# The w_in stage in blocks of 768 tokens instead of 576: matmuls of 384 columns, 24 units, sums of x in place, a new timetable

## The chip, the cores and the metric

The kernel runs on one core of one Trainium2 chip. The metric is the time of one execution on the device, in microseconds (us); of several runs the median counts. Engines: PE is TensorE (PEld its weight loads), DVE VectorE, ACT ScalarE, POOL GpSimd, and SP is SyncE, which in this kernel mostly issues transfers.

## The reference, cut to what matters

Three parts follow one another: linear attention, a mixture of eight experts with one expert for each token, and a dense layer pair with a silu between. The change lies in the first half of the last part.

```python
h = x @ w_in                          # x: 2304 x 512, w_in: 512 x 2048
g = h * (1.0 / (1.0 + np.exp(-h)))
return (g @ w_out).astype(np.float32)  # w_out: 2048 x 512
```

## The kernel before

**Precision.** Every product is computed from two fp32r parts, "high" and "low", of each operand: ScalarE's copy rounds to the high part, VectorE subtracts for the low part. One product of a 128 x 128 weight tile is three matmuls (`three`, L819 to L822: high x high, high x low, low x high).

**Stages.** First comes the attention, then the expert stage in slots s = 0 to 21, each of 128 tokens: `mm1` in four steps, `relu`, a turn through the identity on TensorE (`hturn`), `mm2` in four steps. For each step ScalarE and VectorE split a part of the weights. The outputs of the slots go to the scratch `yd`. Then the w_in stage, and last the w_out stage, which this text calls the drain.

**The w_in stage** multiplies by a scheme like Strassen's, with 7 products for a 2 x 2 split of blocks. The tokens come in 4 blocks k of 2 x TN = 576; the columns of w_in in NJP = 8 pairs q. A unit u = 8k + q is one pair on one block, 32 units in all. Its 7 products (`prod(u, n)`, n from 1 to 7) have six matmuls of TN = 288 columns each. Products 1, 6, 7 and 4 add up in bank puA, 5 and 3 in puC, 2 in puB. After some of the products ScalarE copies puA into an h tile (`keep`, L1121), and VectorE adds puC or puB onto an h tile (`join`, L1128); each finished h tile is stored to the scratch `hd` through SyncE's queue.

A block of x passes through these steps: `xfetch` loads tiles of 128 tokens (on SyncE for tokens in order, on GpSimd by index for the others), `xscale` multiplies by the gate, `xprep` turns a tile by four transposes into one bank and copies it to `xf`; `xsum` builds on VectorE the sums T1n, T2n, T3 and T4 that the scheme needs; `xsplit` is a high part on ScalarE (L1084) and a low part on VectorE (L1088) for each of B11, B21, B22 and T1n to T4. Weights pass through `wfetch` (load), `whigh` (L1015, 1792 elements a partition) and `wlow` (L1019).

**The conversion of w_out** runs beside it. w_out comes as 64-bit floats; `oload` loads one raw tile of 512 KB, `owork` is called four times for the steps that narrow it to 32 bits on VectorE, `okeep` and `osums` build the seven combinations that the drain needs, and `ostore` sends them through GpSimd's queue to the scratch `woscr` (L1195). Later `ofetch` (L1207) loads them from there, and `ohigh` (L1212) and `olow` split them.

**Order.** In this stage each engine works in program order. `unit(u)` issues the products 1 and 5 of u, 4 of u - 1, 6 of u, 3 of u - 1, then 2 and 7 of u. After each, it issues what the timetable `plan()` has put there: `at(u, n, f, ...)` means "after product n in unit u". So "(7,1)" below is the place after product 1 in unit 7. The list `TAIL` is the same for the last expert slot: its entries 0 to 3 are issued with the four steps of mm1 of slot 21, entries 4 to 7 with those of mm2(21). The prods (0,1), (0,5), (0,2), (1,1) and (1,5) follow, and `first_units` has the rest of units 0 and 1. A conditional block, `rest()`, for tokens that don't fit the slots, is skipped on these inputs.

Of the kernel before, what the change touches and what calls it, by code (L numbers as in the profile page):

```python
# [19 lines left out]
P = 128  # L20
# [13 lines left out]
TN = 288  # L34
# [31 lines left out]
def moe_kernel(ctx, tc, qk, v, w_phi, emb, tau, w1, w2, win, wout, out):  # L66
# [193 lines left out]
    def phase_all(ctx):  # L260
# [741 lines left out]
        BK = {}  # L1002

# [37 lines left out]
        def xprep(k, n):  # L1041
            i = tiles_of(k)[n]
            if n == 0:
                XF[k] = [sp.tile([P, 4, TN], F32, name="xf") for _ in range(2)]
# [15 lines left out]
        def xsum(k, name):  # L1060
            b11, b21, b12, b22 = parts(k)
            s = X.setdefault(("s", k), {"B11": b11, "B21": b21, "B22": b22})
            two = lambda nm: b11 if k == 0 else pools["ur"].tile([P, 2, TN], F32, tag="xf2", name="xf2", bufs=2)
            if name == "T1n":
                s[name] = b11
                nc.vector.tensor_tensor(out=b11, in0=b11, in1=b12, op=ALU.subtract)
            elif name == "T3":
                s[name] = b12
                nc.vector.tensor_tensor(out=b12, in0=b22, in1=b12, op=ALU.subtract)
            else:  # L1070
                a, b = (s["T1n"], b22) if name == "T2n" else (s["T2n"], b21)
                s[name] = two(name)
                nc.vector.scalar_tensor_tensor(out=s[name], in0=a, scalar=-1.0, in1=b, op0=ALU.mult,
                                               op1=ALU.subtract)

        def xhigh(k, name):
            if name == "B11":
                pool, tag = (pools["ur"], "xcB") if k % 2 else (sp, "xcA")
            else:
                pool, tag = sp, "xc" + name  # L1080
            s = X.setdefault(("s", k), dict(zip(("B11", "B21", None, "B22"), parts(k))))
            xc = pool.tile([P, 2, 2, TN], F32R, tag=tag, name=tag, bufs=1)
# [7 lines left out]
        def xsplit(k, name):  # L1090
# [75 lines left out]
        def wspot(dt=F32, name="ws"):  # L1166
            return pools["ul"].tile([P, 1536], dt, tag="ws", name=name, bufs=3)

        def oload(j):
            t = wspot(name="wo")  # L1170
            J[NJ + j] = [t[:, 0:1024].bitcast(I32).rearrange("p (f t) -> p f t", t=2), t[:, 1024:1536].bitcast(I32), t]
# [7 lines left out]

        def okeep(m):  # L1180
            ta, tb = J[NJ + m][2], J[NJ + NJP + m][2]
            J["o", m] = {0: ta[:, 1024:1280], 1: tb[:, 1024:1280], 6: tb[:, 1280:1536]}
            ostore(m, 0, 1, 6)

        def osums(m):
            ta, tb = J.pop(NJ + m)[2], J.pop(NJ + NJP + m)[2]
            b11, b12, b21, b22 = (t[:, 1024 + n * 256:1280 + n * 256] for t in (ta, tb) for n in range(2))
# [46 lines left out]
        def gspace0():  # L1234
            for r in range(2):
                gspace(wspot(name="g0"), (0, r))
# [36 lines left out]
        def hspace(t):  # L1273
            if t < 5:
                tags = (("ws", "xcA"), ("xf", "xf"), ("xcT1n", "xcB21"), ("xcT2n", "xcT3"), ("xcT4", "xcB22"))[t]
                two = [wspot(F32R, "hl0") if tag == "ws" else
                       sp.tile([P, 4 * TN], F32R, tag=tag, name="hlx", **({} if tag == "xf" else {"bufs": 1}))
                       for tag in tags]
                HB.append([x[:, 0:1024] for x in two])
# [72 lines left out]
        def rest():  # L1352
            t0, hs = wspot(name="fr0"), wspot(name="fr1")[:, 0:1024]
            t1 = wspot(F32R, "fr2")
            xr, rw = t0[:, 0:512], t0[:, 512:1024]
            ch_, cl_, xh_ = (t1[:, i * 512:(i + 1) * 512] for i in range(3))
            xl_ = pools["ur"].tile([P, 2, TN], F32R, tag="xf2", name="fr3", bufs=2).rearrange("p a t -> p (a t)")[:, 0:512]
            for s in range(NSF, NS):
# [39 lines left out]
                nc.scalar.dma_start(out=yd[bass.ds(r, P), :], in_=xr)  # L1398
        slots = ExitStack()
# [180 lines left out]
        late = ExitStack()  # L1580
        cload(CA)
        cload(CA + 1)
        for s in range(1, NSF + 1):
# [6 lines left out]
            if s < NSF:  # L1590
# [3 lines left out]
                for k in range(4):  # L1594
# [10 lines left out]
                    if k > 1 and 18 <= s < 21 and 2 * (s - 18) + k - 2 < 5:  # L1605
# [12 lines left out]
            if s == 17:  # L1618
# [3 lines left out]
                sp = ctx.enter_context(tc.tile_pool(name="sp", bufs=2, **T))  # L1622
                xfetch(0, 0)
                xfetch(0, 1)
            for i in range(4):
# [12 lines left out]
                if i > 1 and 18 <= s < 21:  # L1638
                    n = 2 * (s - 18) + i - 2
                    if n < 5:  # L1640
                        xprep(0, n)
                        if n < 3:
                            xfetch(0, n + 2)
                    else:
                        xsplit(0, "B11")
            if s < NSF:
                hturn(s)
            if s == NSF - 1:
                xfetch(1, 0)
                xfetch(1, 1)  # L1650
# [13 lines left out]
        pools["ul"] = ctx.enter_context(tc.tile_pool(name="ul", bufs=1, **T))  # L1664
# [11 lines left out]
        def plan():  # L1676
            for q in range(2, NJP):
                at(q - 2, 3 if q == 3 else 6, whigh, q)
                at(*((1, 2) if q == 2 else (q - 1, 5)), wlow, q)
            at(1, 4, wfetch, 6)  # L1680
            at(2, 4, wfetch, 7)
            for k in range(1, NT // (2 * TN)):
                u = NJP * (k - 1)
                for n in range(2 if u else 0):
                    at(u + 1, 1, xfetch, k, n)
                for n, (v, m) in enumerate(((2, 1), (3, 1), (3, 6), (4, 6), (5, 4))):
# [118 lines left out]
```

## Time and profile before

| | before |
|---|---|
| median of 3 runs | 887.43 us (887.1 to 887.65) |
| profiled execution, its own time | 886.14 us |
| its span | 884.4 us |
| granted TensorE clock, mean of the span | 0.998 |
| PE busy | 867.6 us (98%) |
| PEld busy | 794.0 us (90%) |
| DVE busy | 712.0 us (81%) |
| ACT busy | 609.6 us (69%) |
| POOL busy | 287.7 us (33%) |

Busy times are sums over the whole span. The profiled execution is one execution; its time is 1.7 us above its span, and it is 1.3 us under the median of the runs. In the trace the first product of the w_in stage starts at about 500 us, and the drain's first products at about 691 us.

### The profile page before, as it was taken

The page shows a single profiled execution, that of the slowest core. Times are in us where ns is not written, and L with a number is a line of the kernel's source. Part 1 is how long each engine was busy: PE and PEld are TensorE (multiplying, and loading weights), DVE is VectorE, ACT ScalarE, POOL GpSimd, SP SyncE. Part 2 cuts the span into 40 slices and gives each one's busy share as a digit, 9 for nine tenths or more (in the row PEclk, how much of TensorE's full clock was granted, in tenths as well). Part 3 has the DMA queues.
Part 4 walks back from the last instruction along what each step waited for, and adds up shares of the span by engine and source line. Part 5 has one row for each costly group of instructions (what it writes and reads, how often), then busy time and mean ns, then how long its engine had stood idle before and what let it go on. Part 6 is the DMA issues. An engine that isn't in the chain of part 4 may idle for free. (4 is left out here: it accounts for less than half of the span.)

```text
span 884.4 us, 17109 instructions
## 1 busy us (share of the span) xinstructions
PE 867.6 (98%) x6087; PEld 794.0 (90%) x6087; DVE 712.0 (81%) x1165; ACT 609.6 (69%) x999; POOL 287.7 (33%) x298
## 2 busy tenths in 40 slices
PE   8999999999999999999999999999999999999996
PEld 6999999988677778888888899999999999999996
DVE  6888888897898999999988957776765697676761
ACT  6877888746877889889888765444346676656551
POOL 6888887712401523105210021433310001011011
PEclk9999999999999999999999999999999999999999
DMA  6456363449596696877598495788869864726220
GB/s 188 129 141 188 99 186 99 130 132 368 204 238 218 219 252 203 300 247 187 157 369 316 165 304 180 247 289 274 280 211 311 278 170 125 208 76 170 74 81 37
DMA packets 138314, 178.07 MB, mean 201 GB/s; under 512 B 35720, under 2 KB 98824, under 8 KB 138224
## 3 DMA queue, kind: packets, MB, share of 16 engines
q1 hardware_dynamic: 122944, 143.01, 50.9%
q0 software_dynamic: 15200, 33.89, 13.7%
q8 instruction: 49, 0.80, 0.4%
q14 instruction: 41, 0.34, 0.1%
q10 hardware_dynamic: 80, 0.03, 0.0%
HBM read 174.01 MB, written 55.18 MB: 259 GB/s over the span
## 5 line engine op out<-in xcount | busy, mean ns | idle before, releaser
L870 DVE TENSOR_TENSOR wl<-raw,wh 128x1024 fp32r<-128x1024 f32 (+1 forms) x166 | 187.8, 1172 | 19.1 <-ACT wh L869 12.7
L869 ACT CAST wh<-raw 128x1024 fp32r<-128x1024 f32 (+1 forms) x166 | 162.4, 1026 | 20.2 <-PE ph L822 7.6
L1121 ACT COPY ht<-puA 128x288 f32<-128x288 f32 x128 | 50.6, 400 | 80.6 <-PE puA L822 68.4
L447 POOL TENSOR_TENSOR kl<-ke,kh 128x640 fp32r<-128x640 f32 (+1 forms) x52 | 76.7, 1491 | 22.8 <-ACT kh L443 21.7
L820 PE MATMUL ph<-wh,xh 128*128 128x512 f32 x166 | 67.1, 404 | 0.6 <-ACT xh L874 0.6
L822 PE MATMUL ph<-wh,xl 128*128 128x512 f32 x166 | 65.0, 392 | 0.9 <-DVE xl L877 0.9
L821 PE MATMUL ph<-wl,xh 128*128 128x512 f32 x166 | 64.8, 391 | 0.0
L498 PE MATMUL pnx<-kv,qp 128*128 128x73 f32 x512 | 62.3, 275 | 0.0
L822 PE MATMUL pdA<-wod,hlx 128*128 128x256 f32 x216 | 61.2, 283 | 0.6 <-DVE hlx L1287 0.6
L405 DVE TENSOR_REDUCE m<-pqk 128x10 f32<-128x1280 f32 (+1 forms) x32 | 43.4, 1358 | 21.5 <-PE pqk L398 21.3
L498 PEld LDWEIGHTS pnx<-kv,qp 128*128 128x128 f32 x512 | 59.9, 192 | 0.3
L431 ACT ACTIVATE ke<-d 128x640 f32<-128x640 f32 (+1 forms) x52 | 35.6, 684 | 29.9 <-POOL vl L421 15.4
L398 PE MATMUL pqk<-wbd,zh 128*128 128x256 f32 x288 | 53.8, 286 | 1.0 <-DVE d L406 0.9
L1128 DVE TENSOR_TENSOR ht<-puC,ht 128x288 f32<-128x288 f32 x64 | 29.0, 453 | 31.7 <-PE puC L822 25.4
L1195 POOL DMA_DIRECT2D woscr<-wo x56 | 30.8, 557 | 64.3 <-DVE wo L221 61.4
L855 POOL DMA_INDIRECT xg<-xd,gidx x22 | 28.2, 1283 | 68.9 <-PE pxt L890 30.0
L391 POOL TENSOR_TENSOR zl<-z,zh 128x512 fp32r<-128x512 f32 (+1 forms) x29 | 41.6, 1433 | 25.5 <-ACT zh L385 24.6
L820 PE MATMUL pdA<-wod,hlx 128*128 128x256 f32 x176 | 49.8, 283 | 0.0
L821 PE MATMUL pdA<-wod,hlx 128*128 128x256 f32 x176 | 49.8, 283 | 0.0
L1031 POOL DMA_INDIRECT yt<-yd,yidx x13 | 15.2, 1165 | 100.1 <-DMA hd<-ht 69.0
L398 PEld LDWEIGHTS pqk<-wbd,zh 128*128 128x128 f32 x288 | 44.7, 190 | 2.8 <-issue 2.2
L406 DVE TENSOR_TENSOR d<-pqk,m 128x1280 f32<-128x1280 f32 (+1 forms) x32 | 43.5, 1358 | 1.1
(467 smaller groups left out, 3013.2 us busy)
## 6 DMA issues: line engine op xcount, KB each, us to landing
raw<-w SPq DMA_DIRECT2D x44, 1536.0 KB
raw<-w SPq DMA_DIRECT2D x44, 512.0 KB
hd<-ht SPq DMA_DIRECT2D x124, 144.0 KB
wo<-wout SPq DMA_DIRECT2D x16, 512.0 KB
gb<-hd SPq DMA_DIRECT2D x16, 512.0 KB
woscr<-wo POOLq DMA_DIRECT2D x56, 128.0 KB
yd<-ys SPq DMA_DIRECT2D x23, 256.0 KB
z<-qk SPq DMA_DIRECT2D x16, 320.0 KB
```

The source lines that it names most:

```text
L391: eng.tensor_tensor(out=zl, in0=z, in1=zh.bitcast(F32), op=ALU.subtract)
L398: nc.tensor.matmul(out=pqk[:, c * 256:(c + 1) * 256], lhsT=z[:, c * P:(c + 1) * P], rhs=wbd[:, j].rearrange("p h f -> p (h f)"), start=(i ...
L405: nc.vector.tensor_reduce(out=m, in_=pv[:, 0:2 * n], axis=AX.X, op=ALU.max, apply_absolute_value=True)
L406: nc.vector.tensor_tensor(out=d.rearrange("p c s f -> p (c s) f"), in0=pv[:, 0:2 * n], in1=m.unsqueeze(2).to_broadcast([P, 2 * n, F]), op= ...
L447: nc.gpsimd.tensor_tensor(out=kl[:, :, s, :], in0=st.pop(("ke", g, s)), in1=kh[:, :, s, :].bitcast(F32), op=ALU.subtract)
L498: nc.tensor.matmul(out=pn[:, c, 0:73], lhsT=qp[:, s, c * P:(c + 1) * P], rhs=kv[:, s, g % 2, 0:73], start=(s == 0), stop=(s == 1))
L820: nc.tensor.matmul(out=o, lhsT=ah, rhs=bh, start=first, stop=False, skip_group_check=more)
L821: nc.tensor.matmul(out=o, lhsT=ah, rhs=bl, start=False, stop=False, skip_group_check=more)
L822: nc.tensor.matmul(out=o, lhsT=al, rhs=bh, start=False, stop=last, skip_group_check=more)
L869: nc.scalar.copy(out=hi[:, 0:n], in_=sl[:, 0:n])
L870: nc.vector.tensor_tensor(out=lo[:, 0:n], in0=sl[:, 0:n], in1=hi[:, 0:n].bitcast(F32), op=ALU.subtract)
L1121: nc.scalar.copy(out=htile(u, at), in_=BK[u, "A"])
```

## The change

- TN becomes 384: 3 blocks of 768 tokens, 24 units, matmuls of 384 columns. A block of x now is 6 whole tiles.
- `xsum` writes in place: T1n and T4 to one buffer (the one of the raw x tiles, YT), T3 over B12, T2n over B11. Each split part of x has one buffer. `xf` and YT get pools of their own, h tiles are 8 instead of 11.
- The list TAIL and the timetable are written anew. B11 of the first block is split in TAIL and not before; T4 and B22 are split after prods in units 0 and 1.
- The raw tiles of w_out were 3 in rotation; now there is one for each half, and the narrowed parts have three small buffers. `osums` still writes into the raw tile of the second half.
- `rest()` moves from ahead of unit 5 to ahead of unit 2. Block 1 of x was begun in the last expert slot on SyncE and GpSimd; it is now fetched whole in the stage.

```diff
-TN = 288
+TN = 384
 def xfetch(k, n):
-            yt = sp.tile([P, DM], F32, name="yt")
+            yt = YT[0][:, n % 2 * DM:(n % 2 + 1) * DM]
 def xsum(k, name):
-            two = lambda nm: b11 if k == 0 else pools["ur"].tile([P, 2, TN], F32, tag="xf2", name="xf2", bufs=2)
+            aside = YT[0][:, 0:2 * TN].rearrange("p (c t) -> p c t", c=2)
+            s[name] = {"T1n": aside, "T3": b12, "T2n": b11, "T4": aside}[name]
...
 def xhigh(k, name):
-                pool, tag = (pools["ur"], "xcB") if k % 2 else (sp, "xcA")
+            xc = xhome(name).tile([P, 2, 2, TN], F32R, tag="xc" + name, name="xc" + name, bufs=1)
...
-        TAIL = [[(whigh, 0), (xsum, 0, "T1n")], [(wlow, 0), (xsplit, 0, "T1n")], [(xsplit, 0, "B21"), (whigh, 1)],
-                [(xsum, 0, "T2n"), (wlow, 1)], [(xsplit, 0, "T2n"), (xsum, 0, "T3")], [(xsplit, 0, "T3")],
-                [(xsum, 0, "T4"), (xsplit, 0, "T4")], [(xsplit, 0, "B22")]]
+        TAIL = [[(whigh, 0), (xsplit, 0, "B11")], [(wlow, 0), (xsum, 0, "T1n")], [(xsplit, 0, "T1n")],
+                [(xsplit, 0, "B21"), (whigh, 1)], [(wlow, 1), (xsum, 0, "T2n")], [(xsplit, 0, "T2n"), (xsum, 0, "T3")],
+                [(xsplit, 0, "T3")], [(xsum, 0, "T4")]]
...
-                HT[u, at] = pools["ur"].tile([P, TN], F32, tag="h", name="ht", bufs=11)
+                HT[u, at] = pools["ur"].tile([P, TN], F32, tag="h", name="ht", bufs=8)
...
 def wspot(dt=F32, name="ws"):
-            return pools["ul"].tile([P, 1536], dt, tag="ws", name=name, bufs=3)
+            return pools["ul"].tile([P, 1024], dt, tag="ws", name=name, bufs=2)
 def oload(j):
+            if not WS:
+                WS.extend(wspot() for _ in range(2))
+                WS.extend(dspot() for _ in range(3))
+            m, second = j % NJP, j // NJP
+            t = WS[second]
...
         for u in range(2, NUNIT):
-            if u == NJP - 3:
+            if u == 2:
                 more = nc.values_load(regs[0:1, 2, NSF:NSF + 1], min_val=0, max_val=NT + P)
```

The new timetable of `plan()` (the old one stands in the function above):

```python
at(0, 6, xsplit, 0, "T4")
at(1, 6, xsplit, 0, "B22")
for q in range(2, NJP):
    at(*{2: (0, 7), 3: (1, 3)}.get(q, (q - 2, 6)), whigh, q)
    at(*((1, 7) if q == 2 else (q - 1, 5)), wlow, q)
at(1, 4, wfetch, 6)
at(2, 4, wfetch, 7)
for k in range(1, NT // (2 * TN)):
    u = NJP * (k - 1)
    at(u + 2 - k // 2, 1, xfetch, k, 0)
    at(u + 2 - k // 2, 1, xfetch, k, 1)
    for n, (v, m) in enumerate(((3, 1), (3, 6), (4, 1), (4, 6), (5, 1), (5, 6))):
        at(u + v, m, xscale, k, n)
        at(u + v, m, xprep, k, n)
        if n < 4:
            at(u + v, {1: 5, 6: 3}[m], xfetch, k, n + 2)
    for v, m, f, name in ((6, 5, xsum, "T1n"), (6, 3, xsum, "T3"), (7, 1, xsplit, "B11"), (7, 1, xsum, "T2n"),
                          (7, 5, xsplit, "T1n"), (7, 5, xsum, "T4"), (7, 6, xsplit, "T2n"),
                          (7, 2, xsplit, "B21"), (7, 7, xsplit, "T3"), (8, 4, xsplit, "T4"),
                          (8, 3, xsplit, "B22")):
        at(u + v, m, f, k, name)
tiles = [m + NJP * e for m in range(NJP) for e in range(2)]
loads = [(2, 1), (2, 4), (3, 5), (4, 7), (7, 4), (8, 4), (9, 1), (11, 1), (11, 4), (13, 1), (12, 4), (15, 1),
         (16, 6), (17, 5), (17, 6), (18, 7)]
works = [(2, 7), (3, 6), (4, 3), (5, 6), (8, 3), (9, 3), (10, 1), (11, 3), (12, 1), (13, 3), (13, 1), (16, 1),
         (17, 1), (17, 2), (18, 6), (19, 6)]
sums = {0: ((3, 2), (4, 1), (4, 5)), 1: ((5, 2), (6, 1), (6, 5)), 2: ((9, 7), (10, 6), (10, 3)),
        3: ((11, 7), (12, 6), (12, 3)), 4: ((13, 7), (14, 1), (14, 5)), 5: ((16, 4), (16, 2), (16, 7)),
        6: ((17, 7), (18, 5), (18, 4)), 7: ((19, 2), (20, 1), (20, 5))}
# oload at loads[j], four steps of owork from works[j] on, okeep, osums and ostore of the sums at sums[m]
...
for m, p in enumerate(((19, 1), (19, 4), (20, 1))):
    at(*p, ofetch, m, 0)
for m, p in enumerate(((20, 7), (21, 1), (21, 4))):
    at(*p, ofetch, m, 1)
for m in range(3):
    at(21 + m, 1, ohigh, m, 0)
    at(21 + m, 5, olow, m, 0)
    at(21 + m, 6, ohigh, m, 1)
    at(21 + m, 3, olow, m, 1)
...
```

The loads of the drain's first blocks (`gload`) move to units 20 to 22, and its buffers get a pool of their own.

## Rows read from the trace of the kernel before

**Rows 1.** Busy us (x count) by stretch; then granted clock, DMA share, GB/s.
```profile
480.00:500.00 20.00, 20.00 (x103) 16.64 (x102) 19.81 (x21) 18.59 (x25) 0.00 (x0) 1.00 0.65 234
...
560.00:580.00 20.00, 20.00 (x155) 20.00 (x155) 12.37 (x30) 7.77 (x18) 10.71 (x16) 1.00 0.93 306
```
**Rows 2.** Timeline of TensorE, w_in stage: start us, us, engine, line, operation.
```profile
645.03 0.30 PE L820 MATMUL puA<-xcB,wb 128*128 128x288 f32 x1
...
649.83 0.30 PE L820 MATMUL puA<-xcT,wb 128*128 128x288 f32 x1
```
**Rows 3.** Timeline of TensorE, mm2(20), hturn(21), mm2(21) and prod(0,5).
```profile
494.32 0.39 PE L820 MATMUL py<-wh,hh 128*128 128x512 f32 x1
...
497.27 0.39 PE L821 MATMUL py<-wl,hh 128*128 128x512 f32 x1
...
497.73 1.03 PE L922 MATMUL ht<-ident,hs 128*128 128x128 f32 x8
...
500.99 0.40 PE L820 MATMUL po<-wh,hh 128*128 128x512 f32 x1
...
501.46 0.39 PE L822 MATMUL po<-wh,hl 128*128 128x512 f32 x1
...
511.12 0.29 PE L822 MATMUL puB<-xcB,wb 128*128 128x288 f32 x1
...
511.39 0.40 PE L820 MATMUL puA<-xcT,wb 128*128 128x288 f32 x1
```
**Rows 4.** Timeline of VectorE ahead of the stage.
```profile
490.19 2.03 DVE L1019 TENSOR_TENSOR wb<-wb 128x1792 fp32r<-128x1792 f32 x1
...
492.13 0.75 DVE L1088 TENSOR_TENSOR xcT1n<-xf,xcT1n 128x576 fp32r<-128x576 f32 x1
...
496.07 4.62 DVE L870 TENSOR_TENSOR wl<-raw,wh 128x1024 fp32r<-128x1024 f32 x4
...
500.62 1.28 DVE L877 TENSOR_TENSOR hl<-ht,hh 128x512 fp32r<-128x512 f32 x2
```
**Rows 5.** Timeline of ScalarE ahead of the stage.
```profile
488.45 1.71 ACT L1015 CAST wb<-wb 128x1792 fp32r<-128x1792 f32 x1
...
490.26 0.68 ACT L1084 CAST xcT1n<-xf 128x576 fp32r<-128x576 f32 x1
...
491.42 1.69 ACT L1015 CAST wb<-wb 128x1792 fp32r<-128x1792 f32 x1
...
493.02 1.07 ACT L910 ACTIVATE hs<-ph 128x512 f32<-128x512 f32 x2
...
493.98 1.04 ACT L869 CAST wh<-raw 128x1024 fp32r<-128x1024 f32 x1
...
507.31 0.70 ACT L1121 COPY ht<-puA 128x288 f32<-128x288 f32 x2
```
**Rows 6.** Timeline of TensorE around a tile's four transposes.
```profile
562.36 0.29 PE L822 MATMUL puA<-xcB,wb 128*128 128x288 f32 x1
...
562.50 0.60 PE L1048 MATMUL pt<-ident,yt 128*128 128x128 f32 x4
...
562.85 0.38 PE L820 MATMUL puC<-xcT1n,wb 128*128 128x288 f32 x1
...
563.07 0.30 PE L821 MATMUL puC<-xcT1n,wb 128*128 128x288 f32 x1
```
**Rows 7.** Timeline of GpSimd: the stores of one m.
```profile
560.48 2.33 POOL L1195 DMA_DIRECT2D woscr<-wo  x4 [0.56 <-DVE wo L1190]
```
**Rows 8.** Timeline of SyncE: the load of the next raw tile of w_out.
```profile
567.31 0.33 SPq L169 DMA_DIRECT2D wo<-wout  x1
```
**Rows 9.** Waits of SyncE, 562 to 600 us: us in all, times, longest.
```profile
SPq L169 <- DMA woscr<-wo: 1.3, 1, 1.3
```
**Rows 10.** Timeline of SyncE: a load of w_out's combinations.
```profile
664.32 0.88 SPq L1207 DMA_DIRECT2D wob<-woscr  x2
```
**Rows 11.** Timeline of ScalarE: the cast behind that load.
```profile
669.83 1.05 ACT L1212 CAST wob<-wob 128x1024 fp32r<-128x1024 f32 x1 [0.20 <-DMA wob<-woscr]
```

More of the change, by code (lines that the diff above doesn't have):

```diff
@@ L1043, in xprep @@
             if n == 0:
-                XF[k] = [sp.tile([P, 4, TN], F32, name="xf") for _ in range(2)]
+                XF[k] = [xf_pool.tile([P, 4, TN], F32, name="xf") for _ in range(2)]
             yt = X.pop(("y", k, n))
@@ L1234, in gspace0 @@
         def gspace0():
+            ul.close()
+            xf_ctx.close()
+            dl = pools["dl"] = ctx.enter_context(tc.tile_pool(name="dl", bufs=1, **T))
             for r in range(2):
-                gspace(wspot(name="g0"), (0, r))
+                gspace(dl.tile([P, 1024], F32, name=f"g{r}"), (0, r))
+            OSB.extend(dl.tile([P, DM], F32, name=f"os{n}") for n in range(2))
         def gspace1():
@@ L1274, in hspace @@
             if t < 5:
[L1275 to L1279, printed above, removed]
+                homes = (("dl", "dl"), ("dl", "dl"), ("T1n", "B21"), ("T2n", "T3"), ("B11", "dr"))[t]
+                two = [pools[home].tile([P, 1024], F32R, name=f"hl{t}{n}") if home in pools else
+                       sp.tile([P, 4 * TN], F32R, tag="xc" + home, name="hlx", bufs=1)[:, 0:1024]
+                       for n, home in enumerate(homes)]
+                HB.append(two)
             return HB[t % 5]
@@ L1352, in rest @@
         def rest():
-            t0, hs = wspot(name="fr0"), wspot(name="fr1")[:, 0:1024]
-            t1 = wspot(F32R, "fr2")
+            t0, hs = wspot(name="fr0"), wspot(name="fr1")
             xr, rw = t0[:, 0:512], t0[:, 512:1024]
-            ch_, cl_, xh_ = (t1[:, i * 512:(i + 1) * 512] for i in range(3))
-            xl_ = pools["ur"].tile([P, 2, TN], F32R, tag="xf2", name="fr3", bufs=2).rearrange("p a t -> p (a t)")[:, 0:512]
+            ch_, cl_, xh_ = (dspot(F32R, f"fr{i}") for i in range(2, 5))
+            xl_ = xf_pool.tile([P, 2 * DM], F32R, tag="yt", name="fr5", bufs=1)[:, 0:512]
             for s in range(NSF, NS):
@@ L1639, in phase_all @@
                     n = 2 * (s - 18) + i - 2
[L1640 to L1645, printed above, removed]
+                    xprep(0, n)
+                    if n < 4:
+                        xfetch(0, n + 2)
             if s < NSF:
@@ L1691, in plan @@
-                at(u + 4, 2, xsplit, k, "B11")
-                at(u + 5, 2, xsum, k, "T1n")
-                at(u + 6, 5, xsum, k, "T2n")
-                at(u + 6, 6, xsum, k, "T3")
-                at(u + 6, 2, xsum, k, "T4")
-                for v, n, name in ((7, 5, "T1n"), (7, 6, "T2n"), (7, 2, "B21"), (7, 7, "T3"), (8, 4, "T4"), (8, 3, "B22")):
-                    at(u + v, n, xsplit, k, name)
-            units = [u for u in range(6, 25) if u not in (7, 15, 23)]
-            assert len(units) == NJ
@@ new lines, in plan @@
+            for j, ld, (u, n) in zip(tiles, loads, works):
+                at(*ld, oload, j)
+                for e, m in {3: ((0, 3), (0, 3), (0, 2), (0, 2)), 1: ((0, 1), (0, 5), (0, 4), (0, 4)),
+                             6: ((0, 6), (0, 6), (0, 3), (0, 3)), 2: ((0, 2), (0, 2), (0, 7), (0, 7)),
+                             7: ((0, 7), (0, 7), (1, 1), (1, 1))}[n]:
+                    at(u + e, m, owork, j)
+            for m, (k, a, b) in sums.items():
+                at(*k, okeep, m)
+                at(*a, osums, m)
+                at(*b, ostore, m, 2, 3, 4, 5)
@@ L1731, in phase_all @@
+            at(20, 6, gspace0)
+            at(20, 6, gload, 0, 0)
+            at(20, 3, gload, 0, 1)
+            at(20, 7, gspace1)
+            for (u, n), pr in zip(((21, 5), (21, 6), (21, 2), (22, 1)), ((1, 0), (0, 2), (0, 3), (1, 1))):
+                at(u, n, gload, *pr)
+            at(22, 1, ahead, 0)
+            at(22, 5, prepare, 0)
+            at(23, 5, prepare, 1)
+            at(23, 6, ahead, 3)
+            at(23, 2, ahead, 4)
         plan()
@@ L1737, in phase_all @@
                     rest()
+                yspace()
             unit(u, todo)
         prepare(2)
-        OSB.extend(sp.tile([P, DM], F32, tag="yt", name="os") for _ in range(2))
         dprod(0)
```

82 lines of the change are left out of this document (27 added, 55 removed).

## The prediction

> **What bounds the kernel now.** I read the busy time by stretches first, for the stretch that the change rebuilds and the one ahead of it [rows 1]. From 560 to 580 us, in the w_in stage, TensorE is busy for all 20 us, while VectorE works 12.4 us and ScalarE 7.8. From 480 to 500, where the expert stage ends and the first block of x is made ready, VectorE has 19.8 us of work and ScalarE 18.6: there all three are full at once. Then the timeline of TensorE, for the pace. Thirty-six steps of 288 columns take 649.83 - 645.03 = 4.80 us, or 0.1333 us from start to start [rows 2]; thirteen steps of 512 columns take 497.27 - 494.32 = 2.95 us, or 0.2269 [rows 3]. Outside a few gaps of some tenths the stage is this pace and nothing else. So two things decide: how the pace changes with the width, and whether ScalarE and VectorE can still keep their dates under the new order. The timelines of those two engines just before the stage [rows 4, 5] show who waits for whom there.
>
> **The matmuls.** A line through the two widths gives (0.2269 - 0.1333) / 224 = 0.000418 us per column and 0.013 us that a matmul costs whatever its width. At 384 columns that is 0.1333 + 96 x 0.000418 = 0.1734 us. Before there are 32 units of 7 products of 6 matmuls, 1344 x 0.1333 = 179.2 us; after, 24 x 42 = 1008 x 0.1734 = 174.8 us. Gain **4.4 us**. The columns in all stay the same; 336 fixed costs go. The width lies between two measured ones, so I bound the gain by 4.2 and 4.6.
>
> The Trainium skill (TensorE: Matmul & The Clock Gate, Back-to-back issue gap) gives an isolated warm matmul N/2.4 plus about 2.5 ns. By it the fixed part would be 2.5 ns, not 13, and the gain 336 x 0.0025 = 0.8 us. The rows disagree: 288 columns would start every 122.5 ns by it, and they start every 133.3.
>
> **The transposes.** A group of four that turns one tile of x starts at 562.50; the next product starts at 562.85 instead of 562.36 + 0.13, and its second matmul comes 0.22 behind the first, not 0.13 [rows 6]: 0.36 + 0.09 = 0.45 us a group. Blocks of 576 touch 5 tiles each (20 groups), blocks of 768 touch 6 (18 groups). Gain **0.9 us**. The sixth tile of the first block falls into the expert stage, so TensorE comes 0.45 later to the stage's start.
>
> **The start of the stage.** Here the new order costs. Prices first, from occupied steps: VectorE takes 1.94 us for 1792 elements (490.19 to 492.13) and 4.62 / 4 = 1.15 for 1024 [rows 4], so 0.89 for 768 and 0.50 for 384; ScalarE takes 1.60 for 1792 (491.42 to 493.02) and about 0.30 for 288 in the pair at 507.31 [rows 5], so 0.73 for 768, 0.49 for 512, 0.38 for 384.
>
> Before, the sum T1n stands in VectorE's queue ahead of the long wlow(0), so ScalarE's cast of T1n follows its whigh(0) at once, at 490.26 [rows 5]. After, the list TAIL puts the split of B11 first, then wlow(0), and T1n's sum behind it. ScalarE: whigh(0) 488.45 to 490.05, cast of B11 to 490.8. VectorE: low part of B11 to 491.75, wlow(0) to 493.7, sum T1n to 494.6. ScalarE has nothing to do from 490.8 to 494.65. Behind its T1n cast are queued the B21 cast and whigh(1) (0.73 + 0.73 + 1.60): the relu of the last slot starts at 497.7, not 493.02. Then come four casts of w2 at 0.95 (498.75 to 502.55). The first is done at 499.8; VectorE's four low parts take 4.6 more, to 504.35, and the first half of hl(21), before at 500.62 [rows 4], ends at 505.0. TensorE wants that hl in the third matmul of mm2(21), before at 501.46 [rows 3]; with 0.45 for the tile and 18 products' matmuls at 0.04 more each (0.72) it would stand there at 502.6. Loss **2.4 us**, a part of it already at the transposes of hs (497.73 before), which wait for the relu.
>
> A second wait follows on the same chain. wlow(1) and T2n's sum have moved behind hl(21). From its end (505.6): wlow(1) 1.94, sum T2n 0.89, cast 0.73, low 0.89, sum T3 0.89, cast 0.73, then in ScalarE's queue the copy of the last output (0.49) and keep(0,1) (0.38), with about 0.5 for handing over: 513.0. Only then may prod(0,6) add to its bank. TensorE is there after 22 matmuls of 0.227 and 12 of 0.173, at 512.1. Loss **0.9**. Together 3.3; if the queues run 0.3 closer at each link, 2.5, and 4.1 if further apart. The T4 and B22 splits, moved past the start to slots (0,6) and (1,6), are wanted two and three products later and cost nothing if this chain isn't later still. The wait of about 0.14 before xcT at 511.12 to 511.39 [rows 3], with its like, goes: gain **0.2**.
>
> **Slot (7,1).** For blocks 1 and 2, B11 has one buffer, so its cast waits for prod(7,1) and keep(7,1); behind it on VectorE stand B11's low part, T2n's sum, and then join(6,5), which prod(6,3) needs. Needed: 0.2 + 0.38 + 0.73 + 0.89 + 0.89 + 0.50 + 0.2 handing over = 3.8. There: three products, 18 x 0.1734 = 3.1. Loss 0.65, twice: **1.3** (0 if ScalarE is ahead, 1.6 at most).
>
> **The w_out conversion.** Raw tiles were three in rotation; now there is one for each half, and the second also holds the sums until they are stored. For m = 5 these stores stand at (16,7) and the load over them at (17,5), two products later. Four stores take 2.33 us to issue [rows 7]; the last, begun about 562.27, let the next load go at 567.31 [rows 8], which had waited 1.3 us for it [rows 9]: 4.5 us. A load of that size issued at 664.32 [rows 10] let a cast go at 669.83 [rows 11], 5.5 us. From the end of (16,7): sums done 1.15, last store begun 2.8, landed 7.3, load landed 12.8, four conversion steps and join(17,5) 2.45, so 15.3. prod(17,3) wants that join at 11 products, 11.4. Loss 3.8 by these rows; the store with a free queue and the load first in it would halve both, and the loss would be gone. I take **1.5**, nearer the free end because no other tile's store stands in the queue then. SyncE waits at this load, so the stores of h behind it go late too; their tiles are wanted more than a unit (7.3 us) later, and nothing is added. The other loads have four products or more, and their waits on VectorE end before a bank is wanted.
>
> The Trainium skill (Trainium Kernel Development and Optimization, Best Practices) asks to double-buffer so that DMA overlaps with compute. It speaks against this part; the 1.3 us wait with three buffers [rows 9] agrees with it.
>
> **At nothing.** Eight h tiles for eleven: slots freed in order come round after more than a unit, against landings of some us; gone, each late one would hold ScalarE's copies. The conditional block moves from unit 5 to unit 2: its branches cost what they cost before. Block 1 is gathered whole on GpSimd's queue, one unit ahead of its transposes; without that lead each late gather would stop TensorE itself. At the end six casts and the w_out loads share three units of 7.3 us, not five of 5.6; ScalarE already waited 0.2 there [rows 11]; 0 to 2 us, in the range alone.
>
> **The sum.** -4.4 - 0.9 - 0.2 + 2.4 + 0.9 + 1.3 + 1.5 = +0.6 us. The profiled execution took 886.14 (span 884.4 and 1.7 around it), the median of the runs is 887.43; the sum would make them 886.7 and 888.0. About 0.2% (1.8 us) is what can be told from no change.
>
> **The rivals.** (a) Forecast: gain and waits about cancel, 885.7 to 889.2, likeliest 888.0: 0.39. (b) Faster: ScalarE and VectorE make up their queues, the start costs 1 us and the two later waits nothing: -5.5 + 1 gives 882.9, with half of the waits 885: 0.29. For it: 7.6 us of idle VectorE in 20 inside the stage [rows 1]. Against: at the start it has 0.2 idle [rows 1]. (c) Slower: the second raw buffer of w_out decides. If store and load land as in rows 8 to 11, 3.8 instead of 1.5, and the same chain at m = 6 (18,4 to 18,7) and the first load behind the moved branch add about 1: 891.3. It decides from a landing of some 4.5 us for both on. 0.25. (d) The matmuls gain nothing, since the cost of one is all width: 4/3 x 0.1333 = 0.1778 from start to start, the sum 4.4 higher, 892.4: 0.03; the two paces of rows 2 and 3 speak against it. (By the Trainium skill's TensorE: Matmul & The Clock Gate, Back-to-back issue gap, it would come out nearly so.) (e) The end of the stage, its loads drawn together, holds ScalarE 2 us more: 890: 0.04.
>
> Faster is (b), 0.29; slower (c), (d), (e), 0.32; the rest 0.39. The range 883.8 to 891.4 leaves out the far half of (b)'s stretch and the edge of (c) and (d); the forecast's own is 885.7 to 889.2.
>
> **What would show it.** Matmuls of 384 columns starting every 0.173 us, and 72 transposes of x. ScalarE idle for almost 4 us before the T1n cast near 491; relu near 498; TensorE waiting for hl(21) some 2 us near 503 and for keep(0,1) near 512. A gap of 0.6 before puC in units 7 and 15, and one of 0 to 4 us in unit 18 released by VectorE's join. Wrong if the pace isn't 0.173, if ScalarE doesn't wait at T1n, or if the largest gaps are at other places.

## The result, and the profile after

The changed kernel takes 899.14 us (median of 4 runs, 898.48 to 901.08), the kernel before beside it 887.54: a ratio of 1.0129, 95% interval 1.0117 to 1.0141. That is 11.5 us slower, where the prediction said 888.0 and at most 891.4. The profiled execution took 898.48, with a span of 896.8, 12.4 us over that of before.

The page after, its head (busy us, share, instructions):

```profile
span 896.8 us, 16186 instructions
PE 866.7 (97%) x5743; PEld 790.3 (88%) x5743; DVE 709.4 (79%) x1129; ACT 601.6 (67%) x954; POOL 284.8 (32%) x297
```

No engine is busy for longer than before. So the time went into standing still, and a part of it into a slower clock. The windows after, the two of [rows 1] first and then two short ones:

```profile
480.00:500.00 20.00, 19.78 (x99) 16.02 (x98) 14.54 (x17) 15.72 (x21) 0.00 (x0) 1.00 0.65 217
560.00:580.00 20.00, 19.37 (x112) 19.05 (x111) 16.12 (x24) 9.58 (x17) 3.19 (x6) 1.00 0.52 178
524.20:527.40 3.20, 3.20 (x12) 3.20 (x12) 0.81 (x1) 0.48 (x1) 0.00 (x0) 0.50 0.73 275
660.80:663.80 3.00, 3.00 (x11) 3.00 (x11) 2.97 (x7) 0.00 (x0) 1.74 (x4) 0.50 1.00 325
```

The last two have a granted clock of 0.50: TensorE at 1.2 GHz. The waits of TensorE from 496 to 712 us (what it waited for: us in all, times, longest) say where it stood. The kernel before has only 1.0 us of waits in the same view, without the drain's own wait. After:

```profile
PE puC L820 <- DVE ht L1126: 6.1, 5, 2.4
PE puA L820 <- PEq L1759: 2.2, 1, 2.2
PE puA L820 <- ACT ht L1119: 2.0, 3, 0.8
PE pt L1049 <- DMA yt<-yd,yidx: 1.8, 1, 1.8
PE po L822 <- DVE hl L877: 1.2, 1, 1.2
PE pt L1049 <- ACT ht L1119: 0.6, 1, 0.6
PE po L820 <- ACT hh L874: 0.5, 1, 0.5
PE ht L922 <- ACT hs L910: 0.2, 1, 0.2
```

L1759 is the condition of the moved block. The timeline of TensorE after, with the pace (528.86 to 532.85) and the main stops (start, us, operation, idle before it and its releaser):

```profile
503.68 0.40 PE L821 MATMUL po<-wl,hh 128*128 128x512 f32 x1
505.28 0.50 PE L822 MATMUL po<-wh,hl 128*128 128x512 f32 x1 [1.21 <-DVE hl L877]
...
520.53 0.34 PE L822 MATMUL puC<-xcB,wb 128*128 128x384 f32 x1
523.03 0.41 PE L820 MATMUL puA<-xcB,wb 128*128 128x384 f32 x1 [2.16 <-PEq L1759]
...
524.20 0.52 PE L820 MATMUL puC<-xcT1n,wb 128*128 128x384 f32 x1
524.51 0.52 PE L821 MATMUL puC<-xcT1n,wb 128*128 128x384 f32 x1
...
528.86 0.33 PE L820 MATMUL puC<-xcB,wb 128*128 128x384 f32 x1
...
532.85 0.34 PE L822 MATMUL puA<-xcB,wb 128*128 128x384 f32 x1
534.95 0.63 PE L1049 MATMUL pt<-ident,yt 128*128 128x128 f32 x4 [1.76 <-DMA yt<-yd,yidx]
...
656.84 0.34 PE L822 MATMUL puA<-xcT2n,wb 128*128 128x384 f32 x1
659.58 0.44 PE L820 MATMUL puC<-xcB,wb 128*128 128x384 f32 x1 [2.40 <-DVE ht L1126]
```

The pace is 23 steps from start to start in 3.99 us, 0.1735 each (predicted 0.1734). From 524.20 a step takes 0.31 to 0.32; ten of them cost 1.5 us more than at full clock. A stop, counted from start to start less one step, is 2.33 us at 520.53, 1.93 at 532.85, and 2.57 at 656.84.

The account, in us against the profiled execution before: matmuls 1008 x 0.1735 against 1344 x 0.1333, -4.3; transposes -0.9; last expert slot +2.4; keep(0,1) at 512 +0.8; branch at 520 +2.3, half clock behind it +1.5; gathers of block 1, at 533 and 538, +2.7; slots (7,1) and (15,1) +1.6; unit 14, at 625, +1.6; unit 18, at 657, +2.6 and half clock +1.5; end of the stage, at 688 to 706, +2.9; four gaps of the kernel before (0.3 to 0.6 each), which are gone or counted here, -1.8. The sum is +12.9, measured +12.4.

### The profile page after: what moved, and what is told of

It reads as the page before. It is cut to its first block, busy times and chain, and to the rows that moved or that the text cites. A ratio compares the mean times of both kernels' runs of the same rounds, so it can differ in the third digit from the quotient of the medians.

```text
span 896.8 us, 16186 instructions
## 1 busy us (share of the span) xinstructions
PE 866.7 (97%) x5743; PEld 790.3 (88%) x5743; DVE 709.4 (79%) x1129; ACT 601.6 (67%) x954; POOL 284.8 (32%) x297
## 5 line engine op out<-in xcount | busy, mean ns | idle before, releaser
L1119 ACT COPY ht<-puA 128x384 f32<-128x384 f32 x96 | 45.6, 480 | 95.4 <-PE puA L822 89.6
L1032 POOL DMA_INDIRECT yt<-yd,yidx x12 | 13.3, 1106 | 112.9 <-PE puA L822 82.2
L1126 DVE TENSOR_TENSOR ht<-puC,ht 128x384 f32<-128x384 f32 x48 | 26.5, 552 | 27.4 <-PE puC L822 23.1
L822 PE MATMUL pdA<-wod,hl 128*128 128x256 f32 x144 | 40.9, 284 | 0.6 <-DVE hl L1302 0.6
L398 PE MATMUL pqk<-wbd,zl 128*128 128x256 f32 x144 | 40.4, 281 | 0.4 <-DVE zl L391 0.4
L1360 POOL DMA_INDIRECT out<-osd,oidx x10 | 12.7, 1274 | 82.3 <-ACT osd L1351 57.2
L822 PEld LDWEIGHTS ph<-wh,xl 128*128 128x128 f32 x166 | 31.1, 188 | 8.3 <-DVE xl L877 1.5
```

Source lines behind the costliest of these rows:

```text
L398: nc.tensor.matmul(out=pqk[:, c * 256:(c + 1) * 256], lhsT=z[:, c * P:(c + 1) * P], rhs=wbd[:, j].rearrange("p h f -> p (h f)"), start=(i ...
L822: nc.tensor.matmul(out=o, lhsT=al, rhs=bh, start=False, stop=last, skip_group_check=more)
L1119: nc.scalar.copy(out=htile(u, at), in_=BK[u, "A"])
```

## The experiments

All ratios are to the kernel before on the same chip, with 95% intervals; us are medians. "x us less by the ratios" compares a run's ratio with the changed kernel's 1.0129. An expectation weighs theories A, B and at times C; the text names the one that the run bears out.

**1. The conditional block left out.**

```diff
-                more = nc.values_load(regs[0:1, 2, NSF:NSF + 1], min_val=0, max_val=NT + P)
-                with tc.If(more < NT + P):
-                    rest()
```

> The changed kernel without the conditional block ahead of unit 2 (the block, which these inputs skip, is left out with its condition). Theory A (the moved branch is the largest loss: it stops TensorE 2.3 us at 520.5, the clock then runs at half for 3.3 us, and the two gathers of block 1 behind it come late by 1.9 and 0.8): all of that goes, about 6 us, 893 us, and the gathers issue near 524, not 529.3. Theory B (the gathers are late by themselves, one unit ahead is too little): the branch's own 3.6 us go, but gaps before the transposes in unit 3 stay near 1.9 and 0.8; 895.5 us. Theory C (TensorE waits for something else at this place, and the branch is only where it is seen): no change, 899 us.

895.94 us, 1.0085 (1.0066 to 1.0103): 3.9 us less by the ratios. The stop at 520 is gone, and between 515 and 560 only 0.7 us of waiting for a gather is left. So the late gathers hung on the branch: the trace shows A. The time is B's 895.5 all the same, since a gather of block 2 now stops TensorE for 2.0 us at 610, with half clock behind it, and part of the gain is gone again. C falls.

**2. The block moved in the kernel before.**

```diff
-            if u == NJP - 3:
+            if u == 2:
```

> The kernel before with one edit: the conditional block stands ahead of unit 2, not of unit 5. Theory A (the place decides, since the code behind the branch is fetched through the same DMA engines that carry the loads of the weights there): TensorE's branch takes about 3 us, not 0.8, a gap of 1.5 to 2.5 us with a stretch of half clock behind it; 889.5 to 891 us. Theory B (what a branch costs lies in the changed kernel's other code, not in the place): within 0.5 us of the kernel before, 887.5 us.

893.09 us, 1.0062 (1.0045 to 1.0079): 5.3 us slower than the kernel before by this one line, more than A's 889.5 to 891. Here is TensorE's branch (and SyncE's in two of them) in the view of the condition's line: of the kernel before, of the changed kernel, of this run, and of the run with late weight loads (below); x1, then ns, then when:

```profile
L1736 PEldq COMPARE_BRANCH  x1: 785/785/785, 531.4 to 531.4; - x1
```
```profile
L1759 PEldq COMPARE_BRANCH  x1: 3305/3305/3305, 519.6 to 519.6; - x1
L1759 SPq COMPARE_BRANCH  x1: 53/53/53, 522.9 to 522.9; - x1
L1759 SPq EVENT_SEMAPHORE  x9: 17/17/17, 528.1 to 529.5; - x9
```
```profile
L1736 PEldq COMPARE_BRANCH  x1: 4730/4730/4730, 514.3 to 514.3; - x1
```
```profile
L1759 PEldq COMPARE_BRANCH  x1: 1085/1085/1085, 519.9 to 519.9; - x1
L1759 SPq COMPARE_BRANCH  x1: 53/53/53, 522.5 to 522.5; - x1
L1759 SPq EVENT_SEMAPHORE  x9: 17/17/17, 525.2 to 525.8; - x9
```

The same branch over the same block takes 0.8 us at unit 5 and 4.7 at unit 2: the place decides, not the changed kernel's other code (A). SyncE's own branch is short, but its next instruction comes 5.2 us later in the changed kernel. The first gather of block 1 is issued at 529.31, right behind these events.

**3. The sums ahead of the long low parts in TAIL.**

```diff
-        TAIL = [[(whigh, 0), (xsplit, 0, "B11")], [(wlow, 0), (xsum, 0, "T1n")], [(xsplit, 0, "T1n")],
+        TAIL = [[(xsum, 0, "T1n"), (whigh, 0), (xsplit, 0, "B11")], [(wlow, 0), (xsplit, 0, "T1n")],
...
```

> The changed kernel with the sums ahead of the long low parts in TAIL again: T1n's sum first, T2n's sum ahead of wlow(1). Theory A (the prediction's first step: ScalarE idles almost 4 us for the T1n sum, so relu and hl of the last slot are late): the gaps of 0.4, 0.6 and 1.4 us at 498 to 504 go, that of 0.8 at 512 shrinks; 2.4 to 3 us less, 896 to 896.7 us. Theory B (time won there is lost again at the branch and the gathers of units 2 and 3, which wait on other queues): under 1 us less, 898.3 us or more.

896.54 us, 1.0090 (1.0072 to 1.0108): 3.5 us less by the ratios. The stops at 498, 502.5 and 512 are gone, that at 503.7 shrinks from 1.4 to 1.1. The stop at the first transposes of block 1 grows from 1.9 us to 4.9, since TensorE comes there 3.6 us earlier, while the second stop there goes. The slow stretch behind the branch stands behind this stop instead, about as long. A, with a part of B.

**4. Weight loads behind the block.**

```diff
-        wfetch(5)
-            at(1, 4, wfetch, 6)
-            at(2, 4, wfetch, 7)
+            at(2, 1, wfetch, 5)
+            at(2, 4, wfetch, 6)
+            at(3, 4, wfetch, 7)
```

> The changed kernel with the loads of weight pairs 5, 6 and 7 moved behind the conditional block: from ahead of unit 0, (1,4) and (2,4) to (2,1), (2,4) and (3,4). Theory A (the branch waits for its code behind these transfers): TensorE's branch takes about 1 us, not 3.3, the half clock goes with it, and the gathers issue some 2 us earlier; 4 to 6 us less, 893 to 895 us. Theory B (the length of the skip or the branch itself costs 3 us wherever the transfers are): branch still near 3.3 us, 899 us; a late load of weights would show as a gap before unit 5.

The branch takes 1.1 us instead of 3.3, SyncE's skip 2.7 instead of 5.2, and TensorE's stop there is 0.4 us, as A said: the transfers beside the branch set its price. The time did not move: 899.31 us, 1.0132 (1.0115 to 1.0149). The waits of this run from 515 to 545 us show why:

```profile
PE pt L1049 <- DMA yt<-yd,yidx: 4.5, 1, 4.5
PE puA L820 <- PEq L1759: 0.2, 1, 0.2
```

TensorE won 2 us and a slow stretch at the branch, and 0.8 us at the second gather. It stood 2.7 us longer at the first gather, with a slow stretch there that is twice as long. The gathers were issued 2.6 us earlier (526.73 against 529.31), but TensorE could start on the first only 0.75 us earlier, at 534.20: two of the moved loads, of 896 KB each, now leave beside them, at 526.08 and 528.44. A's sum fell: it had counted the links of one chain as separate losses, and the loads that it moved were put beside the next link.

**5. Gathers ahead of the block** (with 3 and 4; the block's scratch moves to another buffer).

```diff
-                at(u + 2 - k // 2, 1, xfetch, k, 0)
-                at(u + 2 - k // 2, 1, xfetch, k, 1)
+                for n in range(2):
+                    at(*((u + 1, 1) if u else (0, 7)), xfetch, k, n)
...
```

> The changed kernel with the order of TAIL and the late weight loads of the two runs before, and the first two gathers of block 1 issued at (0,7), ahead of the conditional block on GpSimd's queue (the block's own scratch moves to a buffer of xf). Theory A (branch and gathers are one chain: SyncE's branch frees the gathers, they come late, TensorE stops there, and its clock falls to half behind the stop; what one link gives up the next takes): with all links moved no gap over 0.8 us is left between 500 and 545 us, and no half clock there; 899.1 - 2.6 (TAIL) - 6.4 (2.3 + 2.7 of gaps, 1.4 of slow clock) = 890, from 889 to 891.5. Theory B (GpSimd's queue or the transfers are late in units 2 to 4 whatever the order): a gap of 2 to 5 us stays at the transposes of unit 3; 894 us or more.

894.82 us, 1.0076 (1.0055 to 1.0097). Branch and gathers stop TensorE for 0.3 us and less. The next link takes the rest: VectorE's queue, with the step on the first w_out tile, which SyncE can load only behind its branch. VectorE in this run:

```profile
531.10 0.43 DVE L206 TENSOR_SCALAR wd<-ws 128x512 f32<-128x512 f32 x1 [5.24 <-DMA ws<-wout]
...
533.29 0.55 DVE L1126 TENSOR_TENSOR ht<-puC,ht 128x384 f32<-128x384 f32 x1
```

The join at 533.29 stands behind it, and TensorE waits 2.6 us for that. The time is B's, but neither theory had this wait; A's chain was one link too short.

**6. Sums of w_out aside.**

```diff
+            tb = YT[0] if m in (5, 6) else tb
-            works = [... (12, 1), (13, 3), (13, 1), ...
+            works = [... (12, 1), (13, 7), (13, 1), ...
-                    4: ((13, 7), (14, 1), (14, 5))
+                    4: ((14, 5), (14, 5), (14, 4))
```

> The changed kernel with the waits of the w_out conversion eased: the sums for m = 5 and 6 go to the buffer of the raw x tiles, which is free then, so the loads at (17,5) and (18,7) wait for no store; the conversion of the second half of m = 4 moves from (13,3) to (13,7), its sums to (14,5). Theory A (rival c of the prediction: one raw buffer for the second half makes the load wait for stores): the gaps of 1.6 us at 625 and 2.6 us at 657 go, with 1.7 us of half clock behind the second; 5 to 6 us less, 893.1 to 894.1 us. Theory B (this is hidden behind the end of the stage, which waits for the last w_out loads anyway): 1 us less or nothing, and larger gaps at 688 to 707.

The first line is for unit 18, the others are for unit 14. 894.27 us, 1.0066 (1.0047 to 1.0084): 5.6 us less by the ratios, as A said. The waits for VectorE's joins from 600 to 680 us, in the changed kernel and in this run:

```profile
PE puC L820 <- DVE ht L1126: 4.4, 3, 2.4
```
```profile
PE puC L820 <- DVE ht L1126: 1.5, 2, 0.9
```

The stop at 625 is gone, that at 657 is down from 2.6 us to 1.1, and no half clock is left at 660. So the mechanism of the prediction's rival (c) is real.

**7. T2n later.**

```diff
-                (7, 1, xsplit, "B11"), (7, 1, xsum, "T2n"), (7, 5, xsplit, "T1n"), (7, 5, xsum, "T4")
+                (7, 1, xsplit, "B11"), (7, 5, xsplit, "T1n"), (7, 5, xsum, "T2n"), (7, 5, xsum, "T4")
```

> The changed kernel with the sum T2n moved from (7,1) to (7,5) behind T1n's split, so that VectorE reaches join(6,5) 0.9 us earlier. Theory A (the prediction's step on slot (7,1)): the gaps of 0.8 us at 570 and 634 go, 1.6 us less, 897.5 us. Theory B (VectorE waits there for ScalarE's cast of B11, not for its own work): the gaps stay over 0.5, 898.7 us.

897.08 us, 1.0108 (1.0088 to 1.0128): 1.9 us less by the ratios, which is not clear of noise by itself, since the intervals overlap. But the stops of 0.8 us at 570 and 634 are gone from the trace. A.

**8. Edits 3 to 7 together.**

> All edits of the runs before together: order of TAIL, late weight loads, gathers ahead of the block, w_out sums aside, T2n later. Theory A (the losses are these places and they add up): 890 - 5.5 - 1.6 = 883, from 881.5 to 885, faster than the kernel before by the gain of the matmuls and the transposes. Theory B (each gap that goes is taken by the next, and in the end by the last stage): 887 us or more.

889.71 us, 1.0014 (1.0003 to 1.0025). Of the 11.5 us, 10.2 are back, but not A's 883 (B). The two longest waits of TensorE from 496 to 712 us:

```profile
PE puC L820 <- DVE ht L1126: 4.2, 4, 2.6
PE puA L820 <- ACT ht L1119: 2.9, 1, 2.9
```

The first is the w_out tile of run 5; the second stands at 677, where ScalarE has the copies of puA queued behind a cast whose load was issued after w_out's last stores. Each is followed by half clock.

**9. First w_out tiles later** (on 8).

```diff
-            loads = [(2, 1), (2, 4), (3, 5), (4, 7), ...
-            works = [(2, 7), (3, 6), (4, 3), (5, 6), ...
+            loads = [(2, 1), (2, 4), (3, 2), (4, 7), ...
+            works = [(3, 6), (3, 2), (4, 7), (5, 6), ...
...
```

> The run with all edits, and the first tiles of w_out converted later: the steps of m = 0 move from (2,7) to (3,6) and those of its second half from (3,6) to (3,2), the load at (3,5) to (3,2); the loads of weight pairs 5 and 6 go behind the first loads of w_out. Theory A (the gap of 2.8 us at 531 that took the place of the late gathers is VectorE waiting for the first w_out tile, which SyncE issues only after its branch): gap and the 1.7 us of half clock behind it go, 889.7 - 4.5 = 885.2, from 884 to 886.5. Theory B (it comes back in unit 4 or at the end of the stage): 888 us or more.

Two weight loads also go behind w_out's first loads. 887.16 us, 0.9995 (0.9984 to 1.0006), between A and B. The stop at 531 is gone, and at 535 TensorE waits 2.2 us for the third gather.

**10. The last w_out tile a unit earlier** (on 9).

> The same, and the last tile of w_out a unit earlier: load from (18,7) to (18,1), steps from (19,6) to (18,7), sums at (19,5), stores at (19,4), and the loads of the combinations' second halves at (20,4), (20,6) and (20,2). Theory A (the gap of 3.1 us at 677 is ScalarE waiting with puA's copy behind a cast whose load was issued at 672, after the last stores): gap and half clock go, 4 us less than without this edit, 880 to 882.5 us, faster than the kernel before by the 5.3 us of matmuls and transposes, and some. Theory B (the transfers at the end are full anyway, the loads land no earlier): 1 us less or nothing.

890.04 us, 1.0026 (1.0013 to 1.0040), against A. The stop at 677, 3.1 us in run 8 but only 0.8 in run 9, is gone, and others at 649, 658 and 683 have grown. The profiled span is only 0.8 us over that of run 9, the median 2.9; what the other executions lost isn't shown.

**11. The transposes of block 1, some loads and the steps for m = 6 later** (on 9).

```diff
+                                           ((3, 1), (3, 6), (4, 6), (5, 1), (5, 6), (6, 1))):
-            at(2, 7, wfetch, 6)
-            at(3, 4, wfetch, 7)
+            at(3, 3, wfetch, 6)
+            at(4, 4, wfetch, 7)
...
```

> The run with the first w_out tiles later, and two dates more: block 1's tiles 2 to 5 are turned one place later each ((4,6), (5,1), (5,6), (6,1)) and the loads of weight pairs 6 and 7 move to (3,3) and (4,4); the steps for the second half of m = 6 move from (17,2) to (17,7), its outputs' stores to (18,1). Theory A (every gap left is one transfer that lands a little after its date, and a stop of over 2 us costs 1.7 us of half clock besides): the gaps of 2.4 us at 535 and 1.5 us at 649 go, with one stretch of half clock; 887.2 - 5.6 = 881.6, from 881 to 884, faster than the kernel before by about the 5.3 us of matmuls and transposes. Theory B (the core's transfers as a whole are the limit in these stretches, and the next one is late instead): 886 us or more.

887.79 us, 0.9991 (0.9976 to 1.0006). The stop moved again, to 546, with 2.1 us of waiting for the fifth gather (B). That gather had been issued behind w_out's stores. GpSimd in this run:

```profile
539.12 1.62 POOL L1207 DMA_DIRECT2D woscr<-ws  x3 [0.51 <-DVE ht L1126]
541.04 1.00 POOL L1032 DMA_INDIRECT yt<-yd,yidx  x1 [0.30 <-issue]
```

**12 to 15. Without w_out's loads, steps and sums.** The first pair, run 12 on run 11 and run 13 on the kernel before, stored zeros in their place:

> The last version of the changed kernel (e11) without w_out's loads, conversion steps and sums (left out: zeros are stored to the scratch at the same places, so the output isn't the reference's). Theory A (what is left of the loss is w_out's pipeline in 24 units instead of 32: its loads crowd the gathers, and VectorE waits for them in order): the gaps at 546 and 649 go with a stretch of half clock, 887.8 - 5 = 882.8, from 881 to 884. Theory B (the gathers or the drain's loads are late by themselves): gaps of over 1 us stay at the transposes, 886 us or more.

> The kernel before without w_out's loads, conversion steps and sums (left out in the same way). Theory A (in the kernel before this pipeline is hidden): 0 to 1.5 us less than the kernel before, 886 to 887.5, and the changed version without it stands 3 to 5 us below, by the matmuls and transposes. Theory B (it costs the kernel before as much): 883 us or less.

891.40 us, 1.0032 (1.0021 to 1.0043), and 895.46, 1.0074 (1.0061 to 1.0088). Neither theory had it: the stores, which no longer wait for VectorE, left in one go. In run 13 GpSimd issued 22 of them in one go, and 29 more behind those, ahead of a gather that it issued only at 577:

```profile
546.10 11.75 POOL L1195 DMA_DIRECT2D woscr<-wo  x22
...
577.37 0.99 POOL L1031 DMA_INDIRECT yt<-yd,yidx  x1 [0.94 <-DMA woscr<-wo]
```

TensorE waited 7.4 us for that gather. So the pair tells nothing of the change, but it shows the price of what stands ahead of a gather. The second pair was to pace the stores, run 14 on run 11 and run 15 on the kernel before:

> The last version of the changed kernel (e11) without w_out's loads, conversion steps and sums; the stores are kept at their dates, each group behind a write of 8 columns by VectorE (zeros are stored, so the output isn't the reference's). Theory A (what is left of the loss is w_out's pipeline in 24 units instead of 32): no gap over 1.3 us and no half clock between 505 and 680 us; 881 to 883.5 us. Theory B (the gathers are late by themselves): gaps of over 2 us stay at the transposes of units 3 to 5, 885 us or more.

> The kernel before without w_out's loads, conversion steps and sums, its stores paced in the same way. Theory A (hidden in the kernel before): 0 to 1.5 us less than the kernel before, 886 to 887.5; the pair's difference is then the change without this pipeline, 4 to 5.3 us. Theory B (it costs the kernel before as much): 883 us or less.

In the changed kernel the stores were not paced: eight left at 524.84 in one go, the third gather at 536.99, and TensorE waited 5.1 us for it; 890.46 us, 1.0024 (1.0012 to 1.0036). In the kernel before they were: 886.41, 0.9984 (0.9975 to 0.9993). There the loads, steps and sums cost 1.4 us (A), or a little more, since run 15 has a wait of 0.9 us for a gather that the kernel before doesn't have.

**16 and 17.** Run 16 is run 11 without w_out's loads, steps and sums, and with all stores (of zeros) in one place, after (14,3). Run 17 is run 11 with the whole pipeline, begun two units later.

> The last version of the changed kernel (e11) without w_out's loads, conversion steps and sums, and with all stores (of zeros, so the output isn't the reference's) in one place after (14,3), behind the last gather. Theory A (w_out's transfers and waits, drawn together into 24 units, eat the gain): no gap over 1.3 us between 505 and 690 us and no half clock there; 880.5 to 883 us. Theory B (the new stage is late at the gathers with no w_out beside it): gaps of over 2 us stay at the transposes of units 3 to 5; 885 us or more.

> The same version with the whole pipeline, begun two units later: m = 0 loaded at (4,1) and (4,4), converted at (5,6) and (5,2), summed at (6,1); m = 1 and 2 follow with less room between them. Theory A: the gap of 2.3 us at 546 (the gather of tile 4 behind w_out's stores on GpSimd) goes, with its half clock; 887.8 - 4 = 883.8, from 882 to 885, faster than the kernel before. Theory B (the wait moves into units 6 to 10): 887 us or more.

Run 16 takes 880.73 us, 0.9914 (0.9895 to 0.9932). The waits of TensorE in it, from 496 to 712 us, all of them but the drain's own:

```profile
PE puC L820 <- DVE ht L1126: 1.0, 1, 1.0
PE po L822 <- DVE hl L877: 0.9, 1, 0.9
...
PE pt L1049 <- ACT xf L1055: 0.3, 1, 0.3
```

That is 5.7 us below run 15, and the matmuls and transposes gain 5.2. The pair isn't quite equal: run 15 keeps the places of its stores and has the wait of 0.9 us named above. Still, the gain is there (A), and w_out's pipeline with its stores eats it. Begun later it eats it elsewhere: run 17 takes 890.40 us, 1.0027 (1.0016 to 1.0039), with six waits for joins, 7.2 us in all (B).

## Why the prediction was wrong, point by point

**Right: the gains.** The pace is 0.1735 against 0.1734, with 18 groups of transposes; run 16 shows the gain in the time. Rival (d) falls: its 0.1778 isn't there. From the figure of the Trainium skill (TensorE: Matmul & The Clock Gate, Back-to-back issue gap) one would estimate 0.1625 us for 384 columns; the measured 0.1735 disagrees.

**Right: the start.** Predicted 2.4 us at mm2(21), measured 0.38 + 0.64 + 1.37 = 2.4. The links stand where they were put, on ScalarE and VectorE after:

```profile
490.21 0.86 ACT L1082 CAST xcB<-xf 128x768 fp32r<-128x768 f32 x1
494.89 0.83 ACT L1082 CAST xcT1n<-yt 128x768 fp32r<-128x768 f32 x1 [3.83 <-DVE yt L1067]
...
497.97 1.06 ACT L910 ACTIVATE hs<-ph 128x512 f32<-128x512 f32 x2
```
```profile
504.55 1.28 DVE L877 TENSOR_TENSOR hl<-ht,hh 128x512 fp32r<-128x512 f32 x2
```

ScalarE idles 3.83 us (predicted almost 4), relu comes at 497.97 (497.7), where [rows 5] had it at 493.02. The stop at keep(0,1) is 0.8 (0.9), those of slot (7,1) are 0.8 each (0.65). Run 3 confirms the start, run 7 slot (7,1), each by the stops that go.

**Wrong: "The conditional block moves from unit 5 to unit 2: its branches cost what they cost before."** This is the step that failed first. I took the cost of a branch for a property of the branch; it belongs to the place and to the transfers there. At unit 2 TensorE's took 3.3 us instead of 0.8: a stop of 2.3 us and 1.5 of half clock, 3.8 in all. SyncE's skip held the gathers, 2.7 more. No rival had a price for it either; (c) counts only a load behind the branch. Run 2 has it alone, 5.3 us; run 4 shows that the transfers beside it set its price. The transfers of 520 to 522 us after, inside TensorE's branch, and of 529.4 to 531.4 before, just ahead of it, each with one packet of code ("instruction"):

```profile
DMA packets 412, 0.70 MB, mean 349 GB/s; under 512 B 48, under 2 KB 389, under 8 KB 411
q8 instruction: 1, 0.02, 3.4%
```
```profile
DMA packets 160, 0.18 MB, mean 88 GB/s; under 512 B 20, under 2 KB 159, under 8 KB 159
q8 instruction: 1, 0.02, 3.0%
```

Before, the packet ran from 529.9 to 530.8 and had ended when the branch began, at 531.4. After, among 349 GB/s, it ran from 520.4 to 521.5, inside the branch of 519.6 to 522.9. The traces of the 18 kernels here that have the block agree. In 13 of them the branch took 0.45 to 1.1 us: the packet had ended 0.3 to 1.3 us ahead of it, and the transfers of the 2 us before it moved 82 to 146 GB/s. In the other five it took 2.6 to 4.7 us: with 276 to 326 GB/s before it the packet began only inside the branch, which ended 1.3 to 1.5 us behind the packet's end. So the branch was long where its code came late among full transfers. That the transfers make the code late, and don't only go with it, rests on run 4.

**Wrong with it: "Block 1 is gathered whole on GpSimd's queue, one unit ahead of its transposes".** The text named what happens without that lead, and costed it at nothing. The gathers' dates were read from the timetable, without asking what else they wait for: SyncE's skip.

**Mis-sized: w_out.** Predicted 1.5 us in unit 18 (3.8 at most), measured 2.6 and half clock, 4.1. The chain stands where it was put. Here are GpSimd's stores for m = 5, SyncE's wait for them with the next load (640 to 660 us), and VectorE's first step on what it loads:

```profile
647.57 2.35 POOL L1206 DMA_DIRECT2D woscr<-ws  x4 [1.06 <-DVE ws L1201]
```
```profile
SPq L169 <- DMA woscr<-ws: 3.0, 1, 3.0
```
```profile
656.84 0.43 DVE L206 TENSOR_SCALAR wd<-ws 128x512 f32<-128x512 f32 x1 [4.22 <-DMA ws<-wout]
```

The load left at 652.71. From the last store's issue, about 649.3, that is 3.4 us, and 4.1 more to the step: 7.5, between the 10 of the prediction's rows and the 5 of its free queue. (Its 4.5 for the store is 5.0 by its own dates, 562.27 to 567.31; the loss by its rows would be 4.3, not 3.8.) "The other loads have four products or more, and their waits on VectorE end before a bank is wanted" failed in unit 14: 1.6 us. Run 6 takes the stop in unit 14 away, and 1.5 us and the half clock of that in unit 18. Rival (c) had the mechanism, and with 3.8 and about 1 most of the 5.7 us measured; its 891.3 was missed by the branch and what hung on it.

**Missing: the clock.** Stops were summed by their length alone. The two longest, of 2.33 and 2.57 us, cost 1.5 us each on top.

**Missing: that covers share their slack.** The end of the stage, "0 to 2 us, in the range alone", took 2.9 us of stops, where the kernel before has 1.0. In runs 4, 5 and 8 to 11 nearly every stop that was taken away came back at another queue. Whether some order of this stage gives the whole gain with w_out beside it stays open: the best of them, runs 9 and 11, can't be told from the kernel before.

## What to carry to other kernels

A step that is moved takes its price from the new place: ask of a branch, a load or a gather what transfers run beside it, and which queue must pass it before the next one is issued. Where one engine is full and three queues in order feed it, do not cost the links of a chain as separate losses: the late ones hide each other, and a fix is worth only the distance to the next. With fewer units and buffers the same side pipeline can cost more: w_out's cost 1.4 us before (run 15) and, with its stores moved too, 7.1 in the new stage (run 16 against run 11). Take it out once, on both kernels, to see whether the gain itself is there.

## What the runs showed of the hardware

TensorE's skipped branch took 0.45 (run 5), 0.79 (before), 1.1 (run 4), 3.3 (after) and 4.7 us (run 2) over the same block, while ScalarE's and VectorE's took 0.05 and 0.07. The Trainium skill (Advanced Engine Details and Errata, Control Flow Timing) gives about 108 ns for a compare and branch; TensorE's rows disagree. The same page of the Trainium skill (ISA Cache) gives cache lines of 16 KB, and the packets of code on queue q8 fit that: 47 of them moved 0.77 MB in the changed kernel.

TensorE's clock fell to 1.2 GHz at the stops of 2.33 and 2.57 us of the changed kernel and not at that of 1.93; in run 11 at one of 2.3, in run 2 at one of 4.3. The length of the stop does not settle it: in run 7 the clock fell at one of 2.0 us (686) and not at one of 2.6 (657), and in run 6 not at one of 2.7 (524), where the granted clock stayed at 1.00. So "a stop of over 2 us costs 1.7 us of half clock", from the expectation of run 11, does not hold in general.
